# Seven half-size products for A11 B11 in experts 2 to 7, single blocks for the sums of h, and another order

## The chip, the core and the metric

The kernel runs on one core of a Trainium2 chip. Its engines work side by side, each through a queue of its own: TensorE (PE; its weight loads are listed apart as PEld), VectorE (DVE), ScalarE (ACT), GpSimd (POOL) and SyncE (SP), which issues most of the transfers. Matmuls write to PSUM, where the kernel holds eight tiles (banks) of 128 x 512 fp32 in the expert part. The metric is the time of one execution on the device in microseconds, as the median of several runs.

## What is computed

Attention with a linear kernel yields x, and a mixture of eight experts with a dense, balanced routing is applied to it:

```
attn_out = linear attention of q, k, v                # 8 x 8 x 576 x 64
x = attn_out.transpose(0, 2, 1, 3).reshape(4608, 512)
P = exp(logits - max)                                 # 4608 x 8, then 8 rounds of row and column scaling
for e in range(8):
    h = np.maximum(x @ w1[e], 0.0)                    # 4608 x 512 times 512 x 1024
    ye = h @ w2[e]                                    # 4608 x 1024 times 1024 x 512
    out += P[:, e:e + 1] * ye
```

The expert part holds most of the work, and nearly all of it is matmul.

## The kernel before

**Tiles and units.** The 4608 rows are cut into nine groups of 512. A unit is one expert on one group; units are numbered 9e + g, so that expert 1 is units 9 to 17 and experts 2 to 7 are units 18 to 71. x is kept transposed in DRAM, ready as tiles `xs` (with the sums T1 to T4 of its blocks); `x_load` fetches the tile of a unit into one of two buffers.

**Seven products instead of eight.** Both layers of a unit are 2 x 2 block products, done by the Winograd form of Strassen's scheme with seven block products: A11 B11, A12 B21, A22 T4, W4 B22, and W1 T1, W2 T2, W3 T3, where W and T are sums and differences of blocks of the two factors. In the first layer A is w1, B is x and the weight sums are `W`; in the second the blocks of h take the place of A, the sums of h are the tile `S` (four blocks), and `T` holds the sums of w2. `combos` makes W and T of an expert on DVE while the expert before it runs.

**First layer.** `block7` (expert 1, and part of expert 0) and `block8` (experts 2 to 7) make h in two pairs a and b, each of 128 x 2 x 256. The products of a pair are called by their numbers: a1 = A11 B11, a2 = A12 B21, a6 = W2 T2, a7 = W3 T3, a3 = W4 B22, a4 = A22 T4, and product 5 is W1 T1. Each is four matmuls of 256 columns. Between them the PSUM results are copied: ACT copies a1's bank into the bank of a2 (`f_seed`, L921), copies partial sums to SBUF (`f_s2`, L925; `f_s5`, L929) and does two of the four relus (L932, L935); DVE does the other two as one add with relu (`addrelu`, L938).

In `block8` product 5 of both pairs is itself cut into 2 x 2 blocks and made by seven products of 128 columns. The groups of matmuls are r1 (products 1 and 5), r6, r7 (products 7, 2 and 3) and r4, all at L868: 4, 2, 6 and 2 matmuls. Between them ACT makes two copies (`f_s`, L876, `f_5`, L880) and DVE two adds (`f_12`, L883, `f_22`, L886). They need the quarter sums of W1 (`U`, made by `w_quarters` on DVE, four per expert) and of T1 (`xf`, made by `x_quarters` on POOL in expert 1, stored to DRAM and fetched by `xf_load`, 128 KB per unit).

**Second layer.** `unit` makes the four sums of h into one tile S of two buffers (L1225), then seven products y1 to y7, each of eight matmuls of 256 columns (L1254), and adds the results, scaled by P, to `acc`. Most results go through `ev` as two operations on DVE that read PSUM (L1285); y2's go through ACT (L1292) into an SBUF tile `st` (three buffers) and from there by an add on POOL (L1295).

**Order.** The program is planned: `_Plan.run` gives every piece of work its place on its engine. The start, up to the first units of expert 2, is a fixed list (`_FRONT`: task numbers with a letter for the engine). For PE the order from expert 1 on is written out in `order`, `order8` and `final` as a pattern per unit; a name such as a7 or r4 means the unit's own product, y a product of the second layer of the unit before. Weights come by POOL's queue, w1 of an expert in two halves, two buffers each.

Of the kernel before, what the change touches and what calls it, by code (L numbers as in the profile page):

```python
# [10 lines left out]
FP32 = mybir.dt.float32  # L11
# [6 lines left out]
class _Plan:  # L18
# [162 lines left out]
    1018p 551d 952p 949d 1019a 552d 992p 1020p 600n 1006n 1011d 5194g 1000p 1021a 703d 1024p 1012d 1001p 1025a 730d  # L181
    5197g 781d 953a 1026p 993a 1022p 668a 1028p 637g 998p 1017n 1023a 1029d 896a 999p 839g 699a 1030p 664a 1004d 1032p
    631g 1013d 1034p 1033a 994p 1035a 633g 1005a 1027d 1038p 1040p 1014d 1039a 1036p 945a 899g 995p 1031a 670d 697a
    1042p 1075p 1037a 780g 1077p 1043d 996p 1078a 666d 1002a 997p 736g 1076a 1044p 1003d 1081p 1045a 1129s 1130m 1528n
    1529g 1530m 1041d 1083p 5195s 5196m 635a 1079p 1046d 1050p 1047d 1052p 1051a 1048d 1082a 1055p 1053d 1049d 1085p
    1056a 1054d 1060p 1058a 1074n 1086d 1057g 1080a 1063p 897g 1062d 1061d 1087p 1064d 1089p 1534n 1535g 1536m 1088a
# [3 lines left out]
    1144p 1122d 5200g 1146p 1148p 1147a 1123p 1149a 701g 1145a 1152p 1125d 1154p 1124d 1153a 1150p 1141d 1531g 1532m  # L190
    1156p 1151a 1189p 1114g 1157d 1191p 1190a 1155d 840g 1126p 1192a 1158p 1128d 1195p 1127d 1159a 1243s 1244m 1197p
    1121d 5198s 5199m 1193p 1160d 5201s 5202m 1164p 1161d 1166p 1162d 1165a 1196a 1169p 1168d 1163d 1199p 1172a 1167d
    1174p 1188n 1194a 1200d 1173g 1170a 1177p 5203g 1175d 1198d 1201p 1176d 1203p 1202a 1205p 5206g 1204a 1180p 1206a
    1209p 1181d 1171g 1211p 1182d 1210a 1207p 783g 1212d 1213p 1208a 1246p 1179d 838a 1248p 1214d 1183p 1247a 1178d
    1249a 732d 1215p 1184d 1252p 1185d 1216a 1300s 1301m 1254p 5204s 5205m 1253a 1217d 1250p 1221p 1245n 1251a 1218d
    1223p 1219d 1222a 1226p 1224d 1220d 1256p 1225d 1231p 1257d 1234p 1233d 1232d 1258p 5209g 1236d 1260p 1533n 1538d
    1262p 1261a 782d 1237p 1263a 1255d 1259a 1266p 1235d 1239d 1268p 1267a 1264p 1227a 1269d 1270p 1265a 1228g 1303p
    1238d 1229a 1305p 1271d 1304a 955g 1240p 1306a 1272p 1241d 1309p 1242d 1273a 1357s 1358m 1311p 5210s 5211m 1310a
    1274d 1307p 5207s 5208m 1278p 1275d 1280p 1276d 1279a 1302n 1308a 1283p 1281d 1277d 1313p 1286a 1282d 1288p 1314d
    1291p 1289d 1290d 1315p 1539d 5212g 1317p 1312d 1319p 1318a 1294p 1293d 1320a 1287g 5213s 5214m 1316a 1323p 1295d  # L200
    1325p 1296d 1324a 1321p 1326d 1327p 1322a 1360p 1292d 1284a 1362p 1328d 1361a 1285g 1297p 1363a 1230g 1329p 1299d
    1366p 1298d 1330a 1414s 1415m 1368p 1331d 1364p 1335p 1359n 1365a 1332d 1337p 1333d 1336a 1367a 1340p 1338d 1334d
    1370p 1339d 1345p 1371d 1348p 1347d 1346d 1372p 1369d 1374p 1349d 1376p 1375a 1537n 1542d 1351p 1377a 1540d 1373a
    1380p 1353d 1382p 1350d 1381a 1378p 1352d 1384p 1541d 1379a 1417p 1385d 1419p 1418a 1383d 1354p 1420a 1341a 1386p
    1356d 1343a 1423p 1355d 1387a 1471s 1472m 1425p 1546d 1388d 1421p 1392p 1547d 1389d 1394p 1390d 1393a 1424a 1397p
    1395d 898a 1391d 1427p 1416n 1422a 1396d 1402p 1400a 1428d 1401g 1405p 1403d 1344g 1404d 1429p 1548d 1426d 954g
    1431p 1433p 1549d 1432a 1408p 1434a 1342g 1430a 1437p 5218g 1410d 1439p 1406d 1438a 1435p 1409d 1441p 1436a 1474p
    1442d 1476p 1475a 1440d 1411p 1398a 1407d 1477a 1399g 1443p 1413d 1480p 1412d 1444a 5215g 1482p 1445d 1478p 1449p
    1446d 1550s 1551m 1451p 1447d 5219s 5220m 1450a 1481a 1454p 1453d 1473n 1479a 1452d 1484p 1448d 1459p 1485d 1462p
    1461d 1543d 1486p 1552s 1553m 1460d 1488p 1463d 1490p 1489a 1483d 1465p 1491a 1464d 1494p 1467d 1496p 1466d 1495a  # L210
    1492p 1457a 1498p 1455a 1458g 1468p 1487a 1499d 1493a 1456g 1497d 1500p 1554p 1470d 2135n 1501a 1615s 2136g 1616m
    2137m 1563p 1469d 5216s 5217m 1555a 1502d 1576p 1556a 1564a 1557p 1506p 1544d 1503d 1566p 1507a 1558d 1508p 1562n
    1567a 1504d 1559p 1577a 1505d 1568p 1565a 1545d 1516p 1569a 1560d 1509d 1570p 1518d 1581p 1517d 1511p 1582a 1571d
    1572p 1617s 1618m 1561p 1522p 1573d 1578a 1510d 1585p 1524d 1579p 1523d 1574p 1586d 1583p 1575a 1525p 1584d 1580a
    1587p 1526d 1519p 1527d 1588a 1680s 1681m 1682s 1683m 1589d 1619p 1628p 1620a 1641p 1590d 1629a 1622p 1593p 1520d
    1621a 1514a 1521d 1512a 1623d 1631p 1515g 1595p 1594a 2138g 2139m 1627n 1632a 1624p 1633p 1625d 1630a 1603p 1591d
    1642a 1634a 1635p 1605d 1646p 1604d 1598p 1596d 1647a 1592d 1637p 1626p 1609p 1638d 1643a 1597d 1650p 1610d 1644p
    1611d 1639p 1651d 1645a 1648p 1599a 1612p 1640a 1649d 1600g 1652p 1613d 1513g 1606p 1614d 1653a 1745s 1746m 1636d
    1747s 1748m 1684p 1693p 1608d 1685a 1706p 1607d 1601a 1694a 1654d 1687p 1658p 1602g 1686a 1688d 1696p 1659a 1655d
    1660p 1692n 1697a 1656d 1689p 1698p 1690d 1695a 1668p 1661d 1707a 1699a 1700p 1669d 1711p 1670d 1663p 1662d 1712a  # L220
    1701d 1702p 1691p 1674p 1703d 1708a 1657d 1666a 1715p 1667g 1676d 1709p 1675d 1704p 1710a 2141n 2142g 2143m 1716d
    1713p 1705a 1677p 1714d 1717p 1679d 1671p 1678d 1718a 1810s 1811m 1812s 1664a 1719d 1749p 1758p 1750a 1673d 1771p
    1751a 1759a 1672d 1752p 1723p 1720d
# [4 lines left out]
def kernel(  # L228
# [53 lines left out]
    xfd = [dpool.tile([P, 512], FP16, tag=f"xf{g}", name=f"xf{g}") for g in range(NG)]  # L282
    wg_sb = const.tile([P, NDT, E], FP16, tag="wg", name="wg_sb")
    P0_sb = const.tile([P, NTT, E], FP32, tag="P0", name="P0_sb")
# [3 lines left out]
    ident = const.tile([P, P], FP16, tag="ident", name="ident")  # L288
    ones_t = const.tile([P, P], FP32, tag="ones", name="ones_t")
# [12 lines left out]
    p_T, p_S, p_W, p_xs, p_xst, p_s2, p_s5 = (S_.pool(2) for _ in range(7))  # L302
    p_st = S_.pool(3)
# [281 lines left out]
    warm = const.tile([P, 512], FP16, tag="warm", name="warm")  # L585
# [193 lines left out]
    def x_quarters(g):  # L779
        gr, td = xs_of[g]  # L780
        gf = S_.grp(p_xf)

        def f_Q(_):
            F = gf["tile"] = accp[2].tile([P, 4, P], FP16, tag="xf", name="xf")
            b11, b12, b21, b22 = (gr["tile"][:, 1536 + P * i:1536 + P * i + P] for i in range(4))
            for i, (a0, a1) in enumerate(((b12, b11), (b22, F[:, 0]), (b22, b12), (b21, F[:, 1]))):
                nc.gpsimd.tensor_tensor(out=F[:, i], in0=a0, in1=a1, op=ALU.subtract)
        t = add(("pool", 1.6), f_Q, deps=[td, x_closed[0]], acq=[gf], use=[gr, gf], prio=NG + g + 0.5)

        def f_sq(_):  # L790
            nc.sync.dma_start(out=xfd[g], in_=gf["tile"].rearrange("p i m -> p (i m)"))
        ti = add(("sp", 0.45), f_sq, deps=[t], use=[gf], prio=NG + g)
        xf_done[g] = add(("dma", 0.9), lambda _: None, deps=[ti], use=[gf], prio=NG + g, lat=2.6)
# [3 lines left out]
    def xf_load(e, g):  # L797
        gr = S_.grp(p_xf)

        def fn(_):  # L800
            gr["tile"] = accp[2].tile([P, 4, P], FP16, tag="xf", name="xf")
            nc.sync.dma_start(out=gr["tile"].rearrange("p i m -> p (i m)"), in_=xfd[g])
        ti = add(("sp", 0.37), fn, acq=[gr], deps=[x_closed[0], xs_prev[0]], prio=e * NG + g)
        xf_issue.append((g, ti))
        xs_prev[0] = ti
        return gr, add(("dma", 0.9), lambda _: None, deps=[ti], use=[gr], prio=e * NG + g, lat=2.6)

    def w_quarters(e, gW, tW):
# [3 lines left out]
        for i in range(4):  # L812
            def f_U(_, i=i):
                if i == 0:
                    gU["tile"] = accp[2].tile([P, 4, 256], FP16, tag="U", name="U")
                A, U = gW["tile"][:, 0], gU["tile"]
                a11, a21, a12, a22 = A[:, 0, 0:256], A[:, 0, 256:512], A[:, 1, 0:256], A[:, 1, 256:512]
                a0, a1, op = [(a21, a22, ALU.add), (U[:, 0], a11, ALU.subtract), (a11, a21, ALU.subtract),
                              (a12, U[:, 1], ALU.subtract)][i]
                nc.vector.tensor_tensor(out=U[:, i], in0=a0, in1=a1, op=op)  # L820
# [601 lines left out]
```

## Time and profile before

| what | value |
|---|---|
| median of 3 runs | 954.0 us (953.99 to 957.35) |
| the profiled execution, its own time | 955.48 us |
| its span, first to last instruction | 953.7 us |
| mean granted TensorE clock | 0.996 |
| transfers | 120.91 MB in the core's packets, HBM read 126.76 MB |

The page gives busy time per engine, the span in slices, the chain of work that ended last, and groups of instructions by line. The slices of the span, in tenths of busy time:

```
PE   7999999999999999999999999999999999999997
DVE  6999899778888988888888888888888888888885
ACT  6999766766555666666666666666666666666663
POOL 6553021664141211111111011111112111111110
```

In the first five slices or so (24 us each) the attention part runs beside expert 0; from about 190 us on the units of experts 1 to 7 follow each other. The end is the last unit's second layer, done without the seven products, and the output transfers.

### The profile page before, as it was taken

What the parts mean: (1) busy time and instruction counts of PE and PEld (TensorE: products, weight loads), DVE (VectorE), ACT (ScalarE), POOL (GpSimd) and SP (SyncE); (2) the same over time, 40 slices, a digit from 0 to 9 for tenths busy, and PEclk for the clock granted to TensorE, in tenths of its full rate; (3) what the DMA queues carried; (4) which work ended last, traced back from release to release, by engine and by line L of the source; (5) the groups of instructions that cost most, each with busy time, mean ns of one, the idle gap of its engine ahead of it and who ended that gap; (6) DMA issues with size and microseconds to landing.
All of it is one profiled execution on the core that took longest, in us unless ns stands there. A gap on an engine that the chain in (4) does not pass through costs nothing.

```text
span 953.7 us, 22986 instructions
## 1 busy us (share of the span) xinstructions
PE 941.9 (99%) x9188; PEld 802.8 (84%) x9188; DVE 813.8 (85%) x1606; ACT 602.2 (63%) x1138; POOL 203.1 (21%) x275
## 2 busy tenths in 40 slices
PE   7999999999999999999999999999999999999997
PEld 3565588788888999999999999999999989999996
DVE  6999899778888988888888888888888888888885
ACT  6999766766555666666666666666666666666663
POOL 6553021664141211111111011111112111111110
PEclk8999999999999999999999999999999999999999
DMA  9999385073225522552227322462225522225555
GB/s 225 245 255 248 91 217 121 18 158 96 92 92 138 131 90 89 134 134 89 90 90 162 106 89 89 113 154 89 89 89 137 131 84 84 81 78 173 173 174 133
DMA packets 54764, 120.91 MB, mean 127 GB/s; under 512 B 5376, under 2 KB 34688, under 8 KB 54656
## 3 DMA queue, kind: packets, MB, share of 16 engines
q1 hardware_dynamic: 30128, 83.83, 26.6%
q0 software_dynamic: 24128, 35.07, 20.0%
q8 instruction: 72, 1.18, 0.5%
q10 hardware_dynamic: 400, 0.52, 0.2%
q14 instruction: 36, 0.29, 0.1%
HBM read 126.76 MB, written 18.87 MB: 153 GB/s over the span
## 4 chain that ended last, share of the span: by engine, by line
PE 98%; DMA 1%; DVE 1%; ACT 0%; issue 0%; POOL 0%; DVEq 0%; ACTq 0%; POOLq 0%
PE ye L1254 36%; PE hq L909 20%; PE Zye L1254 6%; PE R L909 5%; PE Zye L909 5%; PE hq L1011 5%; PE R L868 5%; PE ye L1133 4%; PE hq L692 3%; PE R L1011 2%; PE Zye L1011 1%; PE kv_ps L420 1%; PE att L477 1%; PE att L446 1%; PE yw L597 1%; PE num_ps L477 1%
## 5 line engine op out<-in xcount | busy, mean ns | idle before, releaser
L1285 DVE SCALAR_TENSOR_TENSOR acc<-ye,P_sb,acc 128x256 f32<-128x256 f32 x620 | 272.7, 478 | 56.4 <-PE ye L1254 52.3
L1295 POOL TENSOR_TENSOR acc<-acc,st 128x256 f32<-128x256 f32 x124 | 88.2, 729 | 582.0 <-ACT st L1292 582.0
L1254 PEld LDWEIGHTS <-S 128*128 128x128 f16 x1984 | 191.9, 98 | 21.3
L1254 PE MATMUL ye<-T,S 128*128 128x256 f16 x1488 | 192.8, 273 | 0.0
L1254 PEld LDWEIGHTS <-h 128*128 128x128 f16 x1584 | 152.6, 98 | 16.7
L909 PEld LDWEIGHTS <-w 128*128 128x128 f16 x1296 | 124.5, 98 | 13.6 <-issue 0.2
L909 PEld LDWEIGHTS <-W 128*128 128x128 f16 x1296 | 124.5, 98 | 13.4
L909 PE MATMUL hq<-xs,W 128*128 128x256 f16 x864 | 129.6, 273 | 0.0
L909 PE MATMUL hq<-xs,w 128*128 128x256 f16 x864 | 120.9, 273 | 0.0
L938 DVE CUSTOM_DVE_ANT_0 h<-hq,s 128x512 f16<-128x512 f32 x108 | 74.1, 686 | 33.4 <-PE hq L909 32.9
L925 ACT COPY s<-hq 128x512 f32<-128x512 f32 x108 | 63.6, 589 | 58.9 <-PE hq L909 58.9
L935 ACT ACTIVATE h<-hq 128x512 f16<-128x512 f32 x108 | 64.2, 595 | 57.8 <-PE hq L909 57.8
L932 ACT ACTIVATE h<-Zye 128x512 f16<-128x512 f32 x108 | 64.5, 597 | 52.1 <-PE Zye L909 52.1
L1225 DVE TENSOR_TENSOR S<-h 128x1024 f16<-128x1024 f16 x124 | 85.4, 689 | 9.7 <-ACT h L935 8.8
L938 DVE CUSTOM_DVE_ANT_0 h<-R,s 128x512 f16<-128x512 f32 x108 | 73.7, 682 | 3.8 <-PE R L909 3.7
L1254 PE MATMUL Zye<-w,h 128*128 128x256 f16 x528 | 68.4, 273 | 0.0
L1254 PE MATMUL ye<-w,h 128*128 128x256 f16 x528 | 68.3, 272 | 0.0
L1306 ACT COPY Zye<-ye 128x512 f32<-128x512 f32 x66 | 37.7, 571 | 48.4 <-PE ye L1254 48.4
L1292 ACT ACTIVATE st<-Zye,P_sb 128x256 f32<-128x256 f32 x124 | 52.7, 472 | 21.2 <-PE Zye L1254 21.2
L929 ACT COPY s<-R 128x512 f32<-128x512 f32 x108 | 63.2, 585 | 3.3 <-PE R L868 3.3
L909 PE MATMUL R<-xs,W 128*128 128x256 f16 x432 | 64.8, 273 | 0.0
L909 PE MATMUL Zye<-xs,w 128*128 128x256 f16 x432 | 64.8, 273 | 0.0
(153 smaller groups left out, 1551.8 us busy)
## 6 DMA issues: line engine op xcount, KB each, us to landing
xs<-xd SPq DMA_DIRECT2D x63, 896.0 KB, 4.7
kin<-in_k_dram POOLq DMA_DIRECT2D x15, 576.0 KB, 8.3
out_dram<-acc SPq DMA_DIRECT2D x67, 128.0 KB, 3.7
w<-in_moe_w_dram POOLq DMA_DIRECT2D x16, 512.0 KB, 7.7
xf<-xf SPq DMA_DIRECT2D x63, 128.0 KB, 4.6
w<-in_moe_w_dram POOLq DMA_DIRECT2D x7, 1024.0 KB, 11.7
qin<-in_q_dram POOLq DMA_DIRECT2D x16, 288.0 KB, 8.2
vv<-in_v_dram POOLq DMA_DIRECT2D x16, 288.0 KB, 8.2
```

The costliest lines, as they stand in the source:

```text
L909: nc.tensor.matmul(dst[:, p, :], lhsT=lhs(p, c), rhs=rhs(c), start=(first and p == 0 and c == 0), stop=(c == 1), skip_group_check=True)
L925: nc.scalar.copy(out=gs2["tile"], in_=gX["tile"])
L929: nc.scalar.copy(out=gs5["tile"], in_=gR["tile"])
L932: nc.scalar.activation(out=hd(0, 0), in_=Zt[1], func=AF.Relu)
L935: nc.scalar.activation(out=hd(1, 0), in_=gX["tile"], func=AF.Relu)
L938: nc.vector._custom_dve(TENSOR_ADD_SAT, out=dst, in0=ps, in1=sb, s0=3.0e38, s1=0.0)
L1011: nc.tensor.matmul(dst[:, p, :], lhsT=lhs(p, c), rhs=rhs(c), start=(first and p == 0 and c == 0), stop=(c == 1), skip_group_check=True)
L1225: nc.vector.tensor_tensor(out=Sx[:, i], in0=a0, in1=a1, op=op)
L1254: nc.tensor.matmul(bank(g_)[:, s, :], lhsT=lhs(s, kk), rhs=rhs(kk), start=(new and s == 0 and kk == 0), stop=(kk == 3), skip_group_check=True)
L1285: nc.vector.scalar_tensor_tensor(out=dst(), in0=bank(g_)[:, s, :], scalar=P_sb[:, gg, e:e + 1], in1=dst(), op0=ALU.mult, op1=ALU.add)
L1292: nc.scalar.mul(out=gst["tile"], in_=bank(g_)[:, s, :], mul=P_sb[:, gg, e:e + 1])
L1295: nc.gpsimd.tensor_tensor(out=dst(), in0=dst(), in1=gst["tile"], op=ALU.add)
```

## The change

1. In `block8` A11 B11 of both pairs is made like W1 T1: seven products of 128 columns. The loop over `k` builds the groups x1, x6, x7, x4 (k = 0, from w1, x and new quarter sums) and r1, r6, r7, r4 (k = 1). The four matmul groups a1 and b1 are gone. The x groups use the two `hq` banks that a and b go on with.
2. `U` and `xf` hold quarter sums for both (eight U per expert, `xf` tiles of 256 KB per unit; `x_quarters` works on 128 x 2 x 128 instead of 128 x 128).
3. The sums of h are four tiles of one block each, from five buffers, in the order 2, 0, 1, 3 from expert 2 on; the first of them waits for four of the eight relus only.
4. y3's result goes through ACT and POOL like y2's from expert 2 on; `st` has four buffers.
5. W, T and U of an expert are tied to relus of the expert before (`wd`, and `a22` for U), for experts 3 to 7 one unit earlier than before.
6. The order is written anew: y2 comes two units late, y1 and the rest one unit late, and the entry into expert 2 has a list of its own (`trans`). The end has no list of its own any more. `_FRONT` is new from expert 1 on.
7. Four small tables (P0, ident, ones, warm) move from a pool that lasts to one that is closed after expert 0.

```diff
-    xfd = [dpool.tile([P, 512], FP16, tag=f"xf{g}", name=f"xf{g}") for g in range(NG)]
+    xfd = [dpool.tile([P, 1024], FP16, tag=f"xf{g}", name=f"xf{g}") for g in range(NG)]
...
-    p_T, p_S, p_W, p_xs, p_xst, p_s2, p_s5 = (S_.pool(2) for _ in range(7))
-    p_st = S_.pool(3)
+    p_T, p_S0, p_W, p_xs, p_xst, p_s2, p_s5 = (S_.pool(2) for _ in range(7))
+    p_S = S_.pool(5)
+    p_st = S_.pool(4)
...
         def f_Q(_):
-            F = gf["tile"] = accp[2].tile([P, 4, P], FP16, tag="xf", name="xf")
-            b11, b12, b21, b22 = (gr["tile"][:, 1536 + P * i:1536 + P * i + P] for i in range(4))
-            for i, (a0, a1) in enumerate(((b12, b11), (b22, F[:, 0]), (b22, b12), (b21, F[:, 1]))):
-                nc.gpsimd.tensor_tensor(out=F[:, i], in0=a0, in1=a1, op=ALU.subtract)
+            F = gf["tile"] = accp[2].tile([P, 2, 4, P], FP16, tag="xf", name="xf")
+            v = (gr["tile"][:, 0:3072].rearrange("p (k r) -> p k r", k=2)[:, :, 0:512]
+                 .rearrange("p k (j t m) -> p k j t m", j=2, t=2))
+            b12, b11, b22, b21 = v[:, :, 0, 1], v[:, :, 0, 0], v[:, :, 1, 1], v[:, :, 1, 0]
+            for i, (a0, a1) in enumerate(((b12, b11), (b22, F[:, :, 0]), (b22, b12), (b21, F[:, :, 1]))):
+                nc.gpsimd.tensor_tensor(out=F[:, :, i], in0=a0, in1=a1, op=ALU.subtract)
...
+        for k in range(2):
+            for i in range(4):
+                def f_U(_, i=i, k=k):
...
+                    A = gw1["tile"][:, 0:2, 0:512] if k == 0 else gW["tile"][:, 0]
...
+                at = pe_id.get((NG * (e - 1) + 4 * k + i, "a22")) if e > EQ else None
...
+        def psum(which):
+            return hqp.tile([P, 2, 256], FP32, tag="hq", name="hq") if which == 0 else r_bank()
+        first = []
+        for k in range(2):
+            ga, gb = (S_.grp((p_hq, p_att)[k]) for _ in range(2))
+            nm = "xr"[k]
...
+            t1 = q([(lhs(1, 1), rhs(1, 1), gb, 0), (ul(1), tf(1), gb, 1)], tw1 + [txs, txf, tW, tU, t_zt], [gb], clear=True)
+            ts_ = add(("act", 0.37), f_s, deps=[t1], acq=[ga], use=[gb], prio=ui - 400.0)
+            t6 = q([(ul(2), tf(2), gb, 0)], [ts_])
+            t5 = add(("act", 0.37), f_5, deps=[t1], acq=[gq], use=[gb], prio=ui - 400.0)
+            t12 = add(("dve", 0.42), f_12, deps=[t6, t5], use=[ga, gb, gq], prio=ui - 401.0)
+            t7 = q([(ul(3), tf(3), gb, 0), (lhs(1, 2), rhs(2, 1), ga, 0), (ul(4), rhs(2, 2), ga, 1)], [t12])
+            t22 = add(("dve", 0.42), f_22, deps=[t7], use=[gb, gq], prio=ui - 401.0)
+            t4 = q([(lhs(2, 2), tf(4), gb, 0)], [t22])
...
+            first.append(((ga, t7), (gb, t4)))
...
         def pair(gi):
-            gR, m5 = ((ga, t7), (gb, t4))[gi]
-            gX, gZ, gs2, gs5 = (S_.grp(p) for p in (p_hq, p_ye[3], p_s2, p_s5))
+            (gX, m1), (gR, m5) = first[0][gi], first[1][gi]
+            gZ, gs2, gs5 = (S_.grp(p) for p in (p_ye[3], p_s2, p_s5))
...
-            m1 = pm(A(1, 1, gi), B11, gX, True, tw1 + [txs, prev_hq[0], t_zt], 0.0)
-            prev_hq[0] = m1
...
+    def wd(e, j):
+        if e > EQ:
+            return pe_id.get((NG * (e - 1) + j, "b22"))
+        return pe_id.get((NG * (e - 1) + j + 1, "b22"))
...
+        gS = [S_.grp(p_S0)] * 4 if e == 0 else [S_.grp(p_S) for _ in range(4)]
...
+        for n, i in enumerate((0, 1, 2, 3) if e < EQ else (2, 0, 1, 3)):
...
+            tS[i] = add(("dve", 0.685), f_S, deps=(th_0 if e >= EQ and n == 0 else th_a) + [last_S] + s_free,
+                        acq=[gS[i]] if i == 0 or e > 0 else [], use=[gh, gS[i], gS[i - (i % 2)]], prio=ui - 399.0)
...
-        ev(gR, 0, 1, m3)
+        ev(gR, 0, 1, m3, split=e >= EQ)
...
-    order8 = "r1 a1 b1 r6 y1 a2 y5 r7 a6 y6 a3 b6 y2 a7 r4 y7 b7 b2 a4 b3 y4 b4 y3".split()
-    final = "r1 a1 b1 r6 y1 a2 y5 r7 a6 y6 a3 b6 y2 a7 r4 y7 b7 b2 a4 b3 y3 y4 b4".split()
+    order8 = "x1 r1 y2-- x6 y1- r6 x7 y5- r7 a6 a2 y6- x4 r4 a7 a3 b6 y7- b2 b7 b3 y3- b4 a4 y4-".split()
+    trans = "y1-- b1- y5-- y6-- b6- a7- b5- b2- b7- y7-- a4- b3- b4- y4-- r1 x1 y2-- x6 r6 y3-- x7 r7 y1- a6 a2 a3 x4 y6- y5- r4 b2 b6 a7 y7- b7 b3 y3- a4 b4 r1+ y4- x1+ y2- x6+ r6+ y1 x7+ r7+ y5 a2+ x4+ a6+ r4+ y6 a3+ b6+ b2+ y7 a7+ b7+ b3+ y3 b4+ a4+ y4".split()
```

In the new lists a "-" after a name means the unit before, "--" the one before that, and "+" the unit after.

More of the change, by code (lines that the diff above doesn't have):

```diff
@@ L908, in f_m @@
                         for c in range(2):
-                            nc.tensor.matmul(dst[:, p, :], lhsT=lhs(p, c), rhs=rhs(c),
-                                             start=(first and p == 0 and c == 0), stop=(c == 1), skip_group_check=True)
-                return add(("pe", 0.436), f_m, deps=deps, acq=[g_] if first else [], use=[g_, gw1, gW, gxs],
-                           prio=ui + 0.35 + 0.35 * gi + pr)
+                            nc.tensor.matmul(dst[:, p, :], lhsT=lhs(p, c), rhs=rhs(c), start=False, stop=(c == 1),
+                                             skip_group_check=True)
+                return add(("pe", 0.436), f_m, deps=deps, use=[g_, gw1, gW, gxs], prio=ui + 0.35 + 0.35 * gi + pr)
             def hd(fh, t):
@@ L1245, in bank, with pm @@
             return Zt[0] if g_ is gZ else g_["tile"]
-        def pm(lhs, rhs, g_, new, deps, prio):
+        def pm(lhs, rhs, g_, new, deps, prio, sx=()):
             def f_m(_, e=e):
```

274 lines of the change are left out of this document (137 added, 137 removed).

## The prediction

> **What bounds the kernel now.** I read the page's sums first.
>
> ```profile
> span 953.7 us, 22986 instructions
> PE 941.9 (99%) x9188; PEld 802.8 (84%) x9188; DVE 813.8 (85%) x1606; ACT 602.2 (63%) x1138; POOL 203.1 (21%) x275
> PE 98%; DMA 1%; DVE 1%; ACT 0%; issue 0%; POOL 0%; DVEq 0%; ACTq 0%; POOLq 0%
> ```
>
> TensorE works throughout and is 98% of the chain that ended last. A busy PE is not yet a PE at its peak, so I went to the timeline of one unit of expert 5 (columns: start, length, engine, line, operation).
>
> ```profile
> 601.17 0.28 PE L868 MATMUL R<-xs,W 128*128 128x128 f16 x2
> 601.28 0.27 PE L868 MATMUL R<-xf,U 128*128 128x128 f16 x2
> 601.39 1.04 PE L909 MATMUL hq<-xs,w 128*128 128x256 f16 x8
> 601.59 0.36 ACT L876 COPY R<-R 128x256 f32<-128x256 f32 x1 [0.50 <-PE R L868]
> 601.86 0.38 ACT L880 COPY qs<-R 128x256 f32<-128x256 f32 x1
> 602.29 0.27 PE L868 MATMUL R<-xf,U 128*128 128x128 f16 x2
> 602.40 1.04 PE L1254 MATMUL ye<-w,h 128*128 128x256 f16 x8
> 603.27 0.60 PE L909 MATMUL Zye<-xs,w 128*128 128x256 f16 x4
> ...
> 604.58 0.28 PE L868 MATMUL R<-xf,U 128*128 128x128 f16 x2
> 604.70 0.28 PE L868 MATMUL R<-xs,W 128*128 128x128 f16 x2
> 604.81 0.28 PE L868 MATMUL R<-xs,U 128*128 128x128 f16 x2
> 604.92 0.60 PE L909 MATMUL hq<-xs,W 128*128 128x256 f16 x4
> ...
> 613.33 0.28 PE L868 MATMUL R<-xs,W 128*128 128x128 f16 x2
> ```
>
> The printed lengths overlap; what counts is start to start. Eight matmuls of 256 columns take 602.40 to 603.27; six of 128 columns take 604.58 to 604.92. Over every pair of neighbours from 290 us on, the trace gives 109.15 ns after a 256-column matmul and 55.8 ns after a 128-column one, whatever line follows. A unit repeats every 12.16 us (601.17 to 613.33). It has 104 wide and 14 narrow matmuls: 104 x 0.10915 + 14 x 0.0558 = 12.13 us. So PE has no slack but 0.025 us, and the lines show where: the wide pair at 601.39 should end at 602.27, and r6 starts at 602.29. It waits for the second copy, which ends at 601.86 + 0.38 = 602.24. That repeats in all the units: 53 x 0.025 = 1.33 us. The one other place where PE stands after 150 us is the entry into expert 2, 0.50 us in three gaps (284.38 to 286.24). PE's matmul count sets the end, and only that count, or a new wait on PE, can move it.
>
> How full the others are, for a long stretch inside these experts (columns: busy of PE, weight loads, DVE, ACT, POOL):
>
> ```profile
> 355.00:901.00 546.00, 546.00 (x5303) 491.91 (x5301) 469.32 (x951) 332.98 (x675) 71.28 (x101) 1.00 0.38 111
> ```
>
> DVE 86%, ACT 61%, POOL 13%, DMA 38%, granted clock 1.00.
>
> **The change, part by part.**
>
> *The product A11 B11.* Each of the 54 units of experts 2 to 7 loses m1 of both pairs (8 wide matmuls, 8 x 109.15 = 873 ns) and gets x1, x6, x7, x4 (4 + 2 + 6 + 2 = 14 narrow ones, 14 x 55.8 = 781 ns). That is 0.092 us a unit, 4.99 us in all. The longest row of narrow matmuls so far is six; x1 and r1 now make eight. The Trainium skill, "TensorE: Matmul & The Clock Gate", section "Back-to-back issue gap", speaks against this: it gives about 81 ns for a sustained pair of weight load and 128-column matmul. By it the 14 would cost an estimated 1.13 us, more than the 0.873 removed. The six in a row above take 56 ns each with their weight loads, so the sum goes by 55.8.
>
> *What the seven products bring along, per unit.* ACT: two copies more (0.36 and 0.38). DVE: two adds more (0.42 each). They hide under PE if each result is there when PE comes to it, which I walk through below. Per expert four more U sums on DVE (0.28 each, 0.12 us a unit).
>
> *y3's eviction.* Two DVE operations (pair 0.88 us) become two on ACT (pair 0.84) and two on POOL (0.73 each). So DVE stays as full: 10.45 + 0.84 + 0.12 - 0.88 = 10.5 us of a 12.04 us unit (87%). ACT goes from 7.41 to 9.0 us (75%), POOL from 1.6 to 3.0 (25%). None becomes the bound by its sum.
>
> *Walk through a unit.* Four delays from the lines above: ACT starts 0.20 us after the last matmul's successor would start (601.39 to 601.59); the two copies end 0.85 us after that point (602.24); PE follows its release by 0.05 (602.24 to 602.29); neighbours on ACT and DVE overlap by about 0.1. The new order on PE is x1 r1 y2 x6 y1 r6 x7 y5 r7 a6 a2 y6 x4 r4 a7 a3 b6 y7 b2 b7 b3 y3 b4 a4 y4; y is 0.873 long, a and b 0.437.
> - x6 needs 0.85 + 0.05 = 0.90 after x1; r1 and y2 give 1.10. Slack 0.20. Before, the cover was 0.87: the 0.025 us of stall.
> - r6 comes after its own two copies, 0.54 later than x's; cover 2.08, slack 0.64.
> - x7 waits for a DVE add: 0.20 + 0.42 + 0.05 = 0.67 after x6; y1 and r6 give 0.98. DVE has finished the sum of h ahead of it just in time. Slack 0.3.
> - a6 waits for the seed copy after x7: 0.85; y5 and r7 give 1.21.
> - b6 waits for the seed copy after x4: 0.20 + 0.61 + 0.05 = 0.86; r4, a7, a3 give 0.98. Slack 0.12.
> - The next x1 takes the bank that b4's relu on ACT frees, and that relu now stands behind y3's two evictions. From y3's end: 0.20 + 0.84 + 0.60 + 0.05 = 1.69, or 1.59 with overlap; b4, a4, y4 give 1.75. Slack 0.06 to 0.16.
> - y1 needs bank ye free of the last unit's y4: 0.31 to spare. y7, y3, b4 have 0.4 or more. The sums of h, each in its own block, start after the first four relus and are ready over 1 us before y5.
>
> So no stall in the steady unit: 96 x 0.10915 + 28 x 0.0558 = 12.04 us. r6's 1.33 us come back too, since its cover has grown from 0.87 to 2.08. Bounds: nothing of it back, or one such 0.025 us stall at each of the three tight places (x6, b6, x1), 4.1 us.
>
> *Transfers and POOL.* xf grows from 128 to 256 KB, 54 loads and 9 stores on SP's queue, behind the xs load as before. It lands in 4.6 us now and is asked for a unit ahead, so even doubled it is hidden. The xf sums in expert 1 work on 128x256 instead of 128x128: 0.43 us each now; half of the 128x512 ones of L737 and L739 (1.17 to 1.29) is an estimated 0.62. Nine groups of four: 0.8 to 1.0 us more each, on a POOL that idles in that stage, but st adds and weight loads queue behind it.
>
> *Weight sums and weight load.* W and U of the next expert start a unit earlier. The second half of w1 lands 9.7 to 10.2 us into the first unit; the first W sum comes at about 10.4 on DVE, and the operation that PE needs next is y4's eviction at 12.2. Half a microsecond of cover.
>
> *Entry into expert 2.* The order is new. r1 comes about 2.2 us earlier, because y2 and y3 of the last units move behind it. The xs load for it now waits for PE alone (at 273.4 + 0.2), not for POOL (276.15 before); with 4.7 us to land the last xf store behind it and 2.1 to 2.6 us for the first load (281.28 to 283.40 before), xf is there at about 281.5, r1's part that reads it is due at 283.1. x6 of the first unit has its qs copy behind R's, one 0.27 later, and only y2 as cover: 0.87 against 1.17, a stall of 0.3 us. The 0.50 us of today becomes about 0.3 (bounds 0 to 3 if xf is late).
>
> *At nothing:* the tables moved to another pool (no instruction), the front up to expert 1 (same order on PE), the tail (the last h has y4 and y2, 1.75 us, as cover, so the output follows PE's end as now).
>
> **Sum.** 4.99 + 1.33 + 0.2 = 6.5 us. The profiled execution took 955.48 us, 1.8 around its span of 953.7: span 947.2, time 949.0. The median of the runs is 954.0, 1.5 below that execution, so 947.5; I say 947.6.
>
> **Rivals.**
> 1. *The product counts, the waits don't go.* The tight places (0.06 to 0.2 us) rest on single rows; if each stalls by 0.025 us as r6 did, the gain is 4.99 - 4.1 + 1.33 + 0.2 = 2.4, time 951.6; with one such place, 949. A late xf at the entry costs 1 to 3 us once, 949 to 950.6. For it: today's r6 shows that cover less than 0.03 short stalls every unit. Against: all covers are longer than the needs. 0.19.
> 2. *Slower: ACT's queue becomes the ring.* x1 waits for b4's relu, the relu for y3's evictions, and these for an st buffer that POOL frees; x1 feeds the copies that ACT does next. Each 0.1 us by which the relu is later than the slack costs 5.4 us; from 0.12 us of stall in each unit (0.28 beyond the walk) the change loses. With the relu late by one more ACT operation (0.6), the stall is about 0.45: 0.45 x 54 = 24 against 6.5, time 971. For it: the smallest slack of the walk is here, and ACT rises to 75%. Against: POOL's adds take 1.41 a pair and have 9 us. 0.06.
> 3. *Weight loads no longer hide in the longer rows of narrow matmuls.* Bare, one takes the 98 ns of its row: 28 narrow ones at 98 instead of 55.8 add 1.18 us a unit, 64 us; in the row of eight alone 0.34 a unit, 18 us, time 966. Against: 55.8 in rows of two, four and six alike. 0.03. The 81 ns of the Trainium skill is a milder form of this; by those rows the trace disagrees with it.
> 4. *It doesn't do what it says:* matmuls as many and as wide as before. The built order shows 324 more on PE, so I leave it out.
>
> My forecast has 0.72. This kernel's measurement can tell about 0.5% from no change, 4.8 us. Faster (below 949.2): the forecast and a little of the first rival, 0.74; within 0.5%: 0.18; slower: 0.08. Range 946.6 (stalls all gone, and the 0.3) to 952.0.
>
> **What would show it.** Unit to unit on PE 12.04 us; 55.8 ns after narrow matmuls in rows of eight; no gap ahead of x6, r6, b6, x1; the DVE group of evictions (L1285 now, 478 ns) short of 106 operations (53 units; the last has no y3) and the POOL group of adds (L1295) richer by as many; 0.3 us ahead of the first x6. A unit above 12.1 us proves the walk wrong, and the line ahead of the gap names the rival.

## The result, and the profile after

| | kernel before | changed kernel |
|---|---|---|
| median, 11 runs each, taken together | 957.4 us (953.99 to 960.23) | 961.32 us (956.66 to 963.32) |
| profiled execution, and its span | 955.48, 953.7 us | 962.61, 960.5 us |
| TensorE, from matmul number 1200 to the last one | 835.45 us | 839.31 us |
| time TensorE stands between 150 and 310 us, and behind 310 us | 0.50, 1.33 us | 2.12, 8.42 us |

The change made the kernel slower: ratio 1.0043, 95% interval 1.0022 to 1.0064. I had forecast 947.6 us, that is 6.4 us below the 954.0 that the first three runs gave for the kernel before; its median over eleven runs is 957.4, so 3.4 of the 13.7 us by which the forecast missed lie in that reference.

The third row is the one to compare by. The two programs issue the same TensorE work, in the same order, up to the last unit of expert 1, and yet matmul number 400 (counted without the warm-up) started anywhere from 45.4 to 52.8 us in the eleven profiles of this study. So I count from matmul number 1200 (110.7 to 118.0 us in these profiles) to the last one. The fourth row adds up, over all neighbours on TensorE, what the step from start to start exceeds 109.15 ns (256 columns) or 55.8 ns (128 columns).

The page of the changed kernel:

```profile
span 960.5 us, 24346 instructions
PE 939.3 (98%) x9512; PEld 802.4 (84%) x9512; DVE 834.3 (87%) x1632; ACT 669.6 (70%) x1351; POOL 356.3 (37%) x382
PE 86%; DVE 5%; DMA 5%; ACT 2%; issue 1%; POOL 1%; DVEq 0%; ACTq 0%; POOLq 0%
L1319 POOL TENSOR_TENSOR acc<-acc,st 128x256 f32<-128x256 f32 x230 | 227.4, 1008 | 437.5 <-ACT st L1316 430.2
L1309 DVE SCALAR_TENSOR_TENSOR acc<-ye,P_sb,acc 128x256 f32<-128x256 f32 x514 | 225.2, 477 | 77.9 <-PE ye L1278 42.3
L1248 DVE TENSOR_TENSOR S<-h 128x1024 f16<-128x1024 f16 x124 | 90.4, 729 | 2.0 <-ACT h L1063 0.4
```

In the chain that ended last TensorE fell from 98% to 86%; DVE and transfers took 5% each. POOL's adds became 106 more (230) and DVE's evictions 106 fewer (514), as forecast, but the adds also became longer: 1008 ns each, where most took 727 in the kernel before. The sums of h (L1248) take 729 ns in the mean, where it was 689.

A unit without trouble, TensorE in the timeline (start, length, engine, line, operation):

```profile
569.78 0.27 PE L884 MATMUL hq<-xs,w 128*128 128x128 f16 x2
...
581.82 0.28 PE L884 MATMUL hq<-xs,w 128*128 128x128 f16 x2
581.93 0.28 PE L884 MATMUL hq<-xf,U 128*128 128x128 f16 x2
582.05 0.27 PE L884 MATMUL R<-xs,W 128*128 128x128 f16 x2
582.16 0.28 PE L884 MATMUL R<-xf,U 128*128 128x128 f16 x2
582.27 1.04 PE L1278 MATMUL Zye<-w,h 128*128 128x256 f16 x8
```

Unit to unit it takes 12.04 us (569.78 to 581.82), and the row of eight narrow matmuls takes 0.45 us (581.82 to 582.27), 56 ns each. That is the forecast to the hundredth, in 44 of the 52 steps between units behind 298 us (12.04 or 12.05). The loss is elsewhere. Of the eight other steps, four differ by at most 0.32 us (11.90, 12.21, 12.29, 12.36). The other four, nine units apart, take 13.4 to 14.1 us. They are the second units of experts 3 to 6, where the weights of experts 4 to 7 have just come in. One of them on TensorE:

```profile
520.85 0.28 PE L884 MATMUL hq<-xf,U 128*128 128x128 f16 x2
522.20 1.03 PE L1278 MATMUL ye<-w,h 128*128 128x256 f16 x8 [1.08 <-DVE acc L1309]
523.07 0.28 PE L884 MATMUL R<-xf,U 128*128 128x128 f16 x2
524.03 0.27 PE L884 MATMUL hq<-xf,U 128*128 128x128 f16 x2 [0.68 <-DVE hq L900]
```

In brackets stands the idle time before the instruction and who ended it; it counts from the modelled end of the matmul before, so it is 0.16 us less than the standing time from start to start (1.24 and 0.84 here). y1 waits for an eviction, x7 for an add, both on DVE. Behind 310 us these four pairs of waits make 7.7 of the 8.42 us. DVE at the same place:

```profile
519.37 1.18 DVE L1205 TENSOR_TENSOR W<-w 128x1024 f16<-128x1024 f16 x1 [1.31 <-DMA w<-in_moe_w_dram]
520.48 0.68 DVE L1248 TENSOR_TENSOR S<-h 128x1024 f16<-128x1024 f16 x1
521.08 0.28 DVE L826 TENSOR_TENSOR U<-w 128x256 f16<-128x256 f16 x1
521.29 0.86 DVE L1309 SCALAR_TENSOR_TENSOR acc<-ye,P_sb,acc 128x256 f32<-128x256 f32 x2
522.07 1.56 DVE L1248 TENSOR_TENSOR S<-h 128x1024 f16<-128x1024 f16 x1
523.55 0.42 DVE L900 TENSOR_TENSOR hq<-hq,qs 128x256 f32<-128x256 f32 x1
```

and POOL:

```profile
507.36 0.72 POOL L1319 TENSOR_TENSOR acc<-acc,st 128x256 f32<-128x256 f32 x1
508.03 1.27 POOL L323 DMA_DIRECT2D w<-in_moe_w_dram  x2
...
518.60 1.41 POOL L1319 TENSOR_TENSOR acc<-acc,st 128x256 f32<-128x256 f32 x2 [6.66 <-ACT st L1316]
521.31 0.92 POOL L323 DMA_DIRECT2D w<-in_moe_w_dram  x1 [1.31 <-PE hq L884]
522.26 1.95 POOL L1319 TENSOR_TENSOR acc<-acc,st 128x256 f32<-128x256 f32 x2
```

Read together: the first sum of weights (L1205) stands in DVE's queue and waits 1.31 us for w1. POOL issued that load at 508.03, behind y3's adds, which the change put on this queue; in the unit that I had measured before, it was issued 0.41 us ahead of the unit's first matmul (613.33), now it is 0.5 us behind it (x1 at 507.5). POOL in the kernel before:

```profile
609.47 0.72 POOL L1295 TENSOR_TENSOR acc<-acc,st 128x256 f32<-128x256 f32 x1
612.92 1.27 POOL L321 DMA_DIRECT2D w<-in_moe_w_dram  x2 [2.72 <-PE hq L909]
```

At the four places the sum waits 1.54, 1.31, 0.79 and 0.61 us for w1. Everything behind the sum on DVE is late, y4's eviction first (521.29). And two sums take far longer than 0.68 us, 1.18 and 1.56, each with an add of POOL beside it (518.60, y3's, and 522.26, y2's).

So there were two theories. **Theory L**: w1 lands too late for a sum of weights that now comes a unit earlier. **Theory P**: POOL's adds hold up DVE's sums with two SBUF inputs.

### The profile page after: what moved, and what is told of

Its sections match the earlier page's. It is cut to its first block, busy times and chain, and to the rows that moved or that the text cites. A ratio compares the mean times of both kernels' runs of the same rounds, so it can differ in the third digit from the quotient of the medians.

```text
span 960.5 us, 24346 instructions
## 1 busy us (share of the span) xinstructions
PE 939.3 (98%) x9512; PEld 802.4 (84%) x9512; DVE 834.3 (87%) x1632; ACT 669.6 (70%) x1351; POOL 356.3 (37%) x382
## 4 chain that ended last, share of the span: by engine, by line
PE 86%; DVE 5%; DMA 5%; ACT 2%; issue 1%; POOL 1%; DVEq 0%; ACTq 0%; POOLq 0%
PE ye L1278 32%; PE hq L929 13%; PE Zye L1278 5%; PE Zye L929 5%; PE R L929 5%; DMA w<-in_moe_w_dram 4%; PE hq L1028 4%; PE hq L884 4%; PE R L884 4%; PE ye L1150 4%; PE hq L694 3%; PE R L1028 2%; DVE S L1248 1%; DVE acc L1309 1%; PE Zye L1028 1%
## 5 line engine op out<-in xcount | busy, mean ns | idle before, releaser
L1319 POOL TENSOR_TENSOR acc<-acc,st 128x256 f32<-128x256 f32 x230 | 227.4, 1008 | 437.5 <-ACT st L1316 430.2
L1309 DVE SCALAR_TENSOR_TENSOR acc<-ye,P_sb,acc 128x256 f32<-128x256 f32 x514 | 225.2, 477 | 77.9 <-PE ye L1278 42.3
L1278 PEld LDWEIGHTS <-h 128*128 128x128 f16 x1584 | 150.3, 98 | 20.7 <-issue 5.1
L929 PEld LDWEIGHTS <-W 128*128 128x128 f16 x1296 | 122.2, 98 | 12.5
L929 PEld LDWEIGHTS <-w 128*128 128x128 f16 x864 | 84.3, 98 | 9.9
L1248 DVE TENSOR_TENSOR S<-h 128x1024 f16<-128x1024 f16 x124 | 90.4, 729 | 2.0 <-ACT h L1063 0.4
L1316 ACT ACTIVATE st<-ye,P_sb 128x256 f32<-128x256 f32 x106 | 44.7, 472 | 62.6 <-PE ye L1278 62.6
L884 PEld LDWEIGHTS <-U 128*128 128x128 f16 x864 | 70.8, 98 | 7.7 <-issue 3.7
L940 ACT COPY Zye<-hq 128x512 f32<-128x512 f32 x108 | 62.0, 574 | 20.4 <-ACT h L951 14.1
L1278 PE MATMUL ye<-T,h 128*128 128x256 f16 x496 | 64.3, 273 | 0.4 <-DVE acc L1309 0.4
```

The lines of the kernel that those rows point to most:

```text
L884: nc.tensor.matmul(g_["tile"][:, p, P * t:P * t + P], lhsT=l(p), rhs=r(), start=(clear and n == 0 and p == 0), stop=True, skip_group_check ...
L929: nc.tensor.matmul(dst[:, p, :], lhsT=lhs(p, c), rhs=rhs(c), start=False, stop=(c == 1), skip_group_check=True)
L940: nc.scalar.copy(out=Zt[1], in_=gX["tile"])
L1248: nc.vector.tensor_tensor(out=Sx[i], in0=a0, in1=a1, op=op)
L1278: nc.tensor.matmul(bank(g_)[:, s, :], lhsT=lhs(s, kk), rhs=rhs(kk), start=(new and s == 0 and kk == 0), stop=(kk == 3), skip_group_check=True)
L1309: nc.vector.scalar_tensor_tensor(out=dst(), in0=bank(g_)[:, s, :], scalar=P_sb[:, gg, e:e + 1], in1=dst(), op0=ALU.mult, op1=ALU.add)
```

## The experiments

Where lines moved by two, it is because an edit added lines (L1248 is L1250, L884 is L886, L1319 is L1321). In the code cuts `EQ` is 2, so `e > EQ` means experts 3 to 7. Kernels marked "one" ran once; for them TensorE's stretch from matmul 1200 to the last one and its standing time are compared, not the time.

| kernel | time, us | matmul 1200 to last, us | stands 150 to 310 / behind 310, us |
|---|---|---|---|
| before | | 835.45 | 0.50 / 1.33 |
| changed | | 839.31 | 2.12 / 8.42 |
| e1: W, T, U a unit later | 952.37, median of 10 | 833.21 | 2.31 / 2.09 |
| e2: w1's loads ahead of y3's adds | 957.65, one | 839.27 | 2.37 / 8.12 |
| e3: y3 on DVE again | 961.29, one | 839.50 | 2.01 / 8.78 |
| e4: y3's adds left out | 953.54, one | 835.10 | 2.25 / 4.05 |
| e5: as e1, and w2's load behind y2's adds | 951.14, median of 11 | 831.75 | 2.43 / 0.49 |
| e6: w2's load behind y2's adds alone | 957.35, one | 837.38 | 2.23 / 6.37 |
| e7: as e2, y3's adds as memsets | 952.72, one | 834.61 | 2.05 / 3.78 |
| e8: the kernel before, y3 split as in the change | 984.16, one | 861.33 | 0.50 / 27.21 |
| e9: f_Q's sums as memsets | 968.39, one | 843.40 | 0.72 / 13.88 |

**e1: the sums of weights of experts 4 to 7 one unit later, as before the change**

```diff
-        if e > EQ:
+        if e == EQ + 1:
             return pe_id.get((NG * (e - 1) + j, "b22"))
...
-                at = pe_id.get((NG * (e - 1) + 4 * k + i, "a22")) if e > EQ else None
+                at = pe_id.get((NG * (e - 1) + 4 * k + i + (e > EQ + 1), "a22")) if e > EQ else None
```

> Sums W, T, U of experts 4 to 7 one unit later, as in the kernel before; all else as changed. The changed kernel's profile has 8.4 us of gaps on PE after 310 us: four pairs of about 2.1 us (1.4 in the first), each about 13 us after the first unit of experts 3 to 6 begins. Theory L (DVE stands in its queue at the first W sum until w1 has landed): all four pairs go, gaps after 310 us fall to under 1 us, the span by about 7.5 us. Theory P (the adds of y3 on POOL hold up the sums on DVE, wherever they stand): W still meets the adds, a unit later; the second gap of each pair (1.0 us ahead of x7) stays, and 3 to 4 us of the 8.4 are left.

Against the kernel before (954.41 us in that comparison) the ratio is 0.9981, 0.9956 to 1.0005, which can't be told from no change; the standing time behind 310 us, 2.09 us, is 6.3 us shorter than the changed kernel's and lies between the two expectations (under 1, and 3 to 4). All four pairs of waits are gone. At each place one wait of 0.40 us is left, and it points to the other theory. The timeline at the first of them:

```profile
408.09 0.92 POOL L323 DMA_DIRECT2D w<-in_moe_w_dram  x1 [1.18 <-PE hq L884]
...
409.04 1.42 POOL L1319 TENSOR_TENSOR acc<-acc,st 128x256 f32<-128x256 f32 x2
...
409.34 1.68 DVE L1248 TENSOR_TENSOR S<-h,S 128x1024 f16<-128x1024 f16 x1
...
412.53 0.27 PE L884 MATMUL R<-xf,W 128*128 128x128 f16 x2 [0.24 <-DVE R L903]
```

A load issue (w2's) keeps POOL busy until 409.0, so y2's adds run when the last sum of h wants to start, and that sum takes 1.68 us. r4 waits for what is late behind it.

**e2: w1's loads ahead of y3's adds on POOL's queue**

```diff
+    for e in range(EQ + 2, E):
+        for t in y3_adds[NG * (e - 1) - 2]:
+            S_.dep(t, w_issue[(e, "w1")][-1])
```

> At the same four places POOL issues w1's two loads ahead of y3's adds; all else as changed. Theory L, with POOL's queue as the cause of the late issue: w1 is asked for about 1.2 us earlier and lands as much earlier; the first W sum waits 0 to 0.3 us instead of 1.3, the gap ahead of y1 falls from 1.1 to 1.2 us to under 0.4. Theory P: the adds come later and lie over W and S all the more; the gaps stay at 2 us or grow. If the transfer's own length is the cause (it landed 11.2 us after its issue, against 10.2 before), the gap shrinks by less than half.

The wait for the load is gone and the time is not: 8.12 us of standing. The adds, pushed back, now run in a row of four under a sum of h. One place in the timeline, a unit ahead of the former one:

```profile
504.22 3.25 POOL L1321 TENSOR_TENSOR acc<-acc,st 128x256 f32<-128x256 f32 x4
...
505.79 2.24 DVE L1250 TENSOR_TENSOR S<-S,h 128x1024 f16<-128x1024 f16 x1
...
508.42 0.27 PE L886 MATMUL R<-xf,U 128*128 128x128 f16 x2 [1.13 <-DVE R L902]
```

So the late load is not the only cause: take it away, and the same adds, where this edit puts them, cost as much through the sums.

**e3: y3's eviction of experts 3 to 7 on DVE again**

```diff
-        ev(gR, 0, 1, m3, split=e >= EQ)
+        ev(gR, 0, 1, m3, split=e == EQ)
```

> y3's eviction back on DVE for experts 3 to 7; POOL has half the adds there. The first of the four places still has the adds of expert 2's last unit ahead of the load, the other three don't. L and P together: the first place keeps its 1.2 to 1.4 us, the other three lose most of their 2.1 us (under 0.5 each), and the sums S take 0.68 us again. If neither the queue nor the adds matter: three times 2.1 as before. If DVE (0.88 us more per unit) becomes the bound: units of over 12.04 us away from these places.

No better, 8.78 us. The first place keeps a pair of waits (1.24 and 1.45 us) and the third loses nearly all. The second and fourth were to fall under 0.5 and did not: they still lose 1.47 us each (0.38 ahead of y1, 1.1 ahead of r6, behind sums of h of 2.1 us beside y2's adds). Elsewhere waits of 0.08 to 0.19 us came in, in 13 units (12.22 to 12.24 us instead of 12.04). With y3 back, DVE has no room in this order, which is the third expectation.

**e4: y3's adds on POOL left out in experts 3 to 7** (their part of the output is missing; ACT still evicts)

```diff
                     def f_g(_, gst=gst, dst=dst):
+                        if e > EQ and dh == 1:
+                            return
                         nc.gpsimd.tensor_tensor(out=dst(), in0=dst(), in1=gst["tile"], op=ALU.add)
```

> The adds of y3 on POOL left out for experts 3 to 7 (that part of the result is missing from the output); ACT still makes the scaled copies, DVE has no more work than in the changed kernel. It measures the adds alone. L and P: S 0.68 us instead of 0.73 in the mean, the last three places under 0.5 us each, the first as it is. If DVE's load were the point, e3 and e4 would differ by over 0.3 us at a place.

4.05 us. The first place keeps its pair of waits, which even grew to 1.09 and 1.60 us (there the adds of expert 2's last units are still on the queue), the second has none, the others only the 0.40 at r4. So where y3's adds are gone, 0.8 us are left of 6.3: they carry nearly all of the loss there, by delaying the load or by lying beside sums, and this run can't part the two. It differs from e3 by 1.5 and 1.1 us at the second and fourth places, so by that expectation DVE's load counts as well.

**e7: as e2, but y3's adds are memsets of the `st` tile** (two for each add; the same part of the output is missing)

```diff
+                        if e > EQ and dh == 1:
+                            for c in range(2):
+                                nc.gpsimd.memset(gst["tile"], 0.0)
+                            return
```

> As e2 (w1's loads ahead of y3's adds), but in experts 3 to 7 each of y3's adds on POOL is two memsets of the st tile: POOL is still busy at that place and waits for the same eviction on ACT, but reads nothing from SBUF. Left out of the result: y3's part of experts 3 to 7. Theory P (what holds DVE up is that the add reads SBUF while DVE has a sum with two SBUF inputs): as without the adds (e4), the gaps after 310 us fall from 8.1 to about 4 us or less and the sums of h under the memsets take 0.68 us; time 953.5 us. Rival (it is POOL's queue time, or its writes): gaps stay near 8 us, time 957.7 us.

This one parts them. Two memsets take 0.62 to 0.67 us, nearly as long as an add (0.73), at the same place in the queue, and read nothing. Behind 310 us, 74 sums (L1250, L1207, L1221) have only memsets beside them: mean 685 ns, the longest 694; 18 of them start while a memset runs, and the longest of these takes 689. The 118 that have one of the remaining adds beside them have a mean of 795, the longest 2241. Under a memset it looks like this:

```profile
513.54 0.69 DVE L1250 TENSOR_TENSOR S<-h 128x1024 f16<-128x1024 f16 x1
513.55 1.30 POOL L1323 MEMSET st<- 128x256 f32 x4 [6.65 <-ACT st L1318]
```

The standing time falls from 8.12 to 3.78 us. What holds DVE up is that POOL's operation reads SBUF, not that POOL is busy or writes. The Trainium skill, "SBUF — State Buffer", section "SBUF: two separate sides", has the rule: VectorE, when it has two SBUF inputs, and a GpSimd operation that reads SBUF need the same pair of ports, which one of them holds for its whole instruction while the other waits. By that rule a memset is free, and it was.

**e6 and e5: w2's load behind y2's adds, alone and with e1**

```diff
+    for e in range(EQ + 2, E):
+        S_.dep(w_issue[(e, "w2")][0], y2_adds[NG * (e - 1) - 1][-1])
```

> The changed kernel with the load of w2 behind y2's adds, and nothing else. If each pair of waits at an expert's start has two causes (the first wait, 1.1 to 1.2 us, by w1's late landing and the early sum of weights; the second, 0.8 to 1.0 us, by y2's adds that the issue of w2's load pushes onto the last sum of h), the second ones go and the first ones stay: gaps after 310 us fall from 8.4 to about 4.6 us, and the time from 961.3 to about 957.5 us. If the second wait is only DVE's lateness carried over from the first, both stay: 8.4 us and 961.3 us.

6.37 us of standing, between the two expectations. The first waits of the four pairs stayed (4.69 us in sum, 4.66 in the changed kernel); the second ones fell from 3.01 to 0.95 us in sum. So two thirds of the second waits come from y2's adds being pushed onto the sum of h by the issue of w2's load; the first waits do not.

> Two edits on the changed kernel: the sums of weights of experts 4 to 7 one unit later (as in e1), and the load of w2 issued on POOL's queue behind y2's two adds instead of ahead of them (at 408.1, 516.9, 625.7 and 734.5 us in e1, where the issue takes 0.92 us and pushes the two adds from about 408.4 to 409.0 us, so that they run when the last sum of h wants to start; that sum then takes 1.68 us instead of 0.68). Theory P (an add on POOL that is already running holds up a sum with two SBUF inputs on DVE): the sum takes 0.68 to 0.75 us there, the four waits of 0.40 us at r4 go, TensorE's gaps after 310 us fall from 2.09 to about 0.5 us in sum, and the time is 950.8 us, 1.6 below e1 (its front part varies by 2 us from run to run). Rival (DVE is just too full in these units, whatever POOL does): gaps and time stay at 2.1 and 952.4 us. A second rival: the load now lands 1.7 us later, and the sums of w2 wait for it: new gaps a unit or two later.

0.49 us of standing, as theory P says, and none of the new gaps of the second rival. The former place of the 1.68 us sum:

```profile
516.00 2.30 POOL L1321 TENSOR_TENSOR acc<-acc,st 128x256 f32<-128x256 f32 x2 [1.54 <-ACT st L1318]
...
516.88 0.83 DVE L1250 TENSOR_TENSOR S<-h,S 128x1024 f16<-128x1024 f16 x1
...
518.24 0.92 POOL L323 DMA_DIRECT2D w<-in_moe_w_dram  x1
```

Now POOL is the one that waits: 2.30 us for two adds, and it stands idle for 5.8 us behind the load (519.16 to 524.97). This kernel is faster than the one before: 951.14 against 954.33 us, ratio 0.9958, 0.9939 to 0.9977. By the two ratios (0.9958 / 1.0043) it stands 0.8% below the changed kernel; the two were not run side by side.

**e8: one part of the change alone, y3 through ACT and POOL in the kernel before**

```diff
-        ev(gR, 0, 1, m3)
+        ev(gR, 0, 1, m3, split=e > EQ)
```

> The kernel before with one part of the change alone: y3's eviction of experts 3 to 7 by ACT and POOL instead of DVE. There the sums of weights stand a unit later than in the changed kernel. Theory L (the load decides): w1's late landing has a whole unit of cover, so no unit grows by over 0.3 us, unit 12.16 us, time 954.4 us, within 1.5. Theory P in its strong form (an add beside a sum of h costs by itself): waits of 0.4 to 1.2 us at the starts of experts 4 to 7, as in e1 or more, and 956 us or above.

Both theories missed: 984 us. From the third unit of expert 3 on each unit takes 12.76 us, with one wait of 0.63. ACT and TensorE in the timeline:

```profile
510.60 0.84 ACT L1292 ACTIVATE st<-ye,P_sb 128x256 f32<-128x256 f32 x2 [0.34 <-PE ye L1254]
511.32 0.39 ACT L876 COPY R<-R 128x256 f32<-128x256 f32 x1
511.62 0.38 ACT L880 COPY qs<-R 128x256 f32<-128x256 f32 x1
...
512.06 0.27 PE L868 MATMUL R<-xf,U 128*128 128x128 f16 x2 [0.47 <-ACT qs L880]
```

In that order y3 is the last product of a unit, so its evictions stand on ACT ahead of the copies that r6 waits for. ACT's queue is what my second rival feared, though by another step (there it was b4's relu), and it is real where y3 is last. The changed kernel puts y3 ahead of b4, a4 and y4 and has no such wait; that this place in the order is the reason is argued, since no run moves y3 alone. On POOL this run decides nothing: sums of h beside its adds take 2.1 us at three places behind w2's issue, but r6's wait hides them.

**e9: the sums of the half blocks of x in `f_Q` as memsets** (their values are missing in experts 2 to 7)

```diff
-                nc.gpsimd.tensor_tensor(out=F[:, :, i], in0=a0, in1=a1, op=ALU.subtract)
+                nc.gpsimd.memset(F[:, :, i], 0.0)
```

> The changed kernel, with the sums of the half blocks of x in f_Q (L791, POOL, 128x256, four for each half column) replaced by memsets of the same tiles: POOL reads nothing there. Left out of the result: the values of those sums, in experts 2 to 7. It is about the 2.12 us of TensorE's gaps between 150 and 310 us (0.50 in the kernel before), where f_Q runs in expert 1 with DVE's sums of h at 1.00, 1.04 and 1.21 us. Theory P (POOL's reads of SBUF hold up the two-input sums): the gaps at 233 and 239 us (1.01 in sum) and the one at 277 us (0.39) go; the one at x6 of the first unit of expert 2 (0.64, a copy on ACT) and the 0.08 behind it stay: 0.7 to 0.9 us in sum, and after 310 us everything as in the changed kernel (8.4 us). Time about 960 us. Rival (the order of the instructions in expert 1, searched anew, puts DVE behind whatever POOL reads): 2.0 to 2.2 us, as in the other variants.

In expert 1 as expected: 0.72 us between 150 and 310 us, only x6's two waits left. The changed kernel there:

```profile
228.22 0.68 POOL L791 TENSOR_TENSOR xf<-xs 128x256 f16<-128x256 f16 x1
228.44 1.00 DVE L1248 TENSOR_TENSOR S<-h 128x1024 f16<-128x1024 f16 x1
228.84 1.12 POOL L791 TENSOR_TENSOR xf<-xs,xf 128x256 f16<-128x256 f16 x1
229.47 1.04 DVE L1248 TENSOR_TENSOR S<-S,h 128x1024 f16<-128x1024 f16 x1
229.93 1.17 POOL L1319 TENSOR_TENSOR acc<-acc,st 128x256 f32<-128x256 f32 x1
230.44 1.21 DVE L1248 TENSOR_TENSOR S<-h 128x1024 f16<-128x1024 f16 x1
```

and the same three sums with memsets, which ended at 227.5 here:

```profile
230.28 0.69 DVE L1248 TENSOR_TENSOR S<-h 128x1024 f16<-128x1024 f16 x1
231.01 0.69 DVE L1248 TENSOR_TENSOR S<-S,h 128x1024 f16<-128x1024 f16 x1
231.62 0.68 DVE L1248 TENSOR_TENSOR S<-h 128x1024 f16<-128x1024 f16 x1
```

The memsets are also shorter (0.26 against 0.67 us), and nothing of POOL runs beside these three sums, so this run doesn't part reading from being busy. e7 does, for y3's adds; for these sums the same cause is inferred. Behind 310 us I had expected no difference, and there was one: 13.88 us instead of 8.42. Three of the four second waits were 1.59 instead of 0.84 to 1.00 (the first was 1.00 instead of 0.16), behind a sum of h of 2.31 us. At the third place it ended 0.56 us after the second of y2's adds (635.95 to 636.51), in the changed kernel 0.63 us after the first (633.47 to 634.10). Right behind two of these waits TensorE's matmuls came at half their rate for some 3 us (granted clock 0.93 over the 25 us around), which makes about 3 of the 5.5 us. Why the same program point cost more in this run stays open.

## Why the prediction was wrong, point by point

**The product A11 B11, 4.99 us.** Right (4.97 by the rounded figures shown). Rows of eight narrow matmuls run at 56 ns each, so the third rival is out. So is, for this kernel, the 81 ns that the Trainium skill gives in "TensorE: Matmul & The Clock Gate", section "Back-to-back issue gap".

**r6's wait, 1.33 us, and the walk through a unit.** Right: 12.04 us. Outside the entry into expert 2 and the units around a weight load only one of the tight places (x6, b6, x1) stalled, and once: 0.17 us ahead of x1 at 899.53, behind the relu on ACT that follows y3's evictions, where the walk had its smallest slack. My first rival did not happen. But the walk was of a unit in which no weights are loaded, and every slack on DVE in it was reckoned with sums of 0.68 us.

**"Weight sums and weight load ... Half a microsecond of cover."** This step failed, by its first number. The landing, 9.7 to 10.2 us into the unit, was taken from the kernel before, where POOL's queue had only y2's adds; in the changed kernel w1 landed 11.1 to 12.0 us into it. The time at which DVE comes to the first W sum was right (10.55 us, forecast 10.4). Of the 1.6 us of lateness in the mean, 0.9 is the issue behind y3's adds (without them, from the second place on in e3 and e4, it goes out 0.4 us ahead of the unit again). The rest is a longer transfer, 11.0 instead of 10.3 us in the mean from the first issue to the second landing (at the place shown 11.25, 508.03 to 519.28; in the kernel before 10.61, 503.50 to 514.11). The doubled `xf` transfers are a possible reason for that, which no run tests. The half microsecond became a wait of 0.6 to 1.5 us on DVE, with y4's eviction and all the rest behind it. I had costed the move of the sums to an earlier unit, and the move of y3, and never put the two on one queue. Undoing the move alone (e1) brings 6.3 of the 8.42 us back.

**"None becomes the bound by its sum."** True and beside the point. POOL was not the bound (forecast 25%, measured 35% between 355 and 901 us), but its adds read SBUF beside DVE's sums. I costed y3's adds with 0.73 us on POOL and nothing on DVE: a term put at nothing. e2 and e7 show that they cost a sum of DVE up to 1.6 us where they fall badly. The same holds for y2's adds, which the new order puts beside the sums of h: they are two thirds of the second waits (e6), and the 1.6 us by which e5 stands less than e1. The row for it was missing in the trace of before: behind 298 us only 3 of 210 sums of h had an add beside them there, and none of the three was longer for it (681 to 692 ns).

**"Transfers and POOL".** TensorE never waited for `xf` itself (what it may do to w1's transfer stands above), and f_Q's operations took 0.67 us against my 0.62. What I left out is again DVE: by e9 they cost 1.4 us of waits in expert 1 (2.12 to 0.72).

**Entry into expert 2, about 0.3 us.** The place was right (x6 behind its copy on ACT), the size was 0.64 and 0.08 us; why it is more than 0.3 is not shown.

**The sum.** By the profiles from matmul 1200 on: 835.45 - 4.99 - 1.33 - 0.50 + 2.12 + 8.42 = 839.2 us, measured 839.31. The gain was there in full and was given back with 4 us on top. With both repairs (e5) the stretch is 831.75, 3.7 us below the kernel before; what it still lacks are mostly the 2.43 us of waits around expert 1.

**The rivals.** My slower case was ACT's queue. e8 shows the mechanism at work in another order, 0.63 us a unit, but the changed kernel was slowed by DVE, at four places and not in each unit. The step that I feared, the relu behind y3's evictions, held TensorE up once, by 0.17 us. POOL stood in that rival only as the engine that frees `st`; no rival had its queue delay a weight load, or its reads hold up DVE. I had given "slower" 0.08.

## What to carry to other kernels

When work moves onto an idle engine, ask two things that its busy share doesn't answer: which transfers does it issue behind that work, and which operations of other engines it holds up while it reads. When an edit makes a consumer earlier and another makes its producer later, walk both on one time axis; here the later load alone cost nothing (e1), the earlier sums alone waited at most 0.5 us from the second place on (e3 and e4), and the two together 0.6 to 1.5 us. And walk the special units (first of an expert, with its loads) as well as the steady one: 44 of 52 steps were as forecast, and four decided.

## What was not expected of the hardware

- **POOL's adds and DVE's two-input sums.** In the changed kernel behind 310 us, adds that start while a sum runs take 1.15 us on average (151 of them), the 23 with no sum beside them 0.73. Mostly it is POOL that waits, and that costs nothing. Sums alone take 682 ns (24 of them, at most 693); with an add beside them up to 1.72, and 2.31 in e9. By the section of the Trainium skill named above, the one that starts first keeps the ports. The 151 adds agree, and so do 125 of the 129 sums that start ahead of an add (at most 694 ns). The other four don't, and they are the ones behind the second waits: 0.88, 1.56, 1.72 and 1.72 us, though by the record they start 0.19 to 0.35 us ahead of the add (the sum at 522.07 is one).
- **What those four sums have in common.** Each starts while POOL issues w2's load, with the add right behind the issue. The issue alone lengthens nothing: 20 sums of the kernel before, the changed kernel and e6 that start during an issue with no add behind it take 676 to 693 ns. In all the runs, behind 310 us, a sum that starts ahead of its add by the record is longer than 0.7 us only where it starts like these four. Why the add gets the ports there stays open.
- **Evictions are free of it.** DVE's evictions, with one input in PSUM and one in SBUF, are not lengthened (476.6 ns in the mean with an add beside them, 477.4 without).
- **The front differs between runs of the same instructions.** TensorE's matmul number 400 starts between 45.4 and 52.8 us, ahead of anything that the change touches on TensorE. Runs of one kernel differ about as much in time (6.2 us for the kernel before, 6.7 for the changed one). From matmul 400 to 1200 ten of the eleven profiles agree to 0.02 us (e6 takes 1.8 us more), and a stretch measured from number 1200 has none of this.
